# Attention and FFN on one core: one round of sums for block 3, merged score bursts in blocks 0 to 2, and a new load order for batch 3

## The chip, the cores and the metric

The kernel runs on one core of a Trainium2 chip. The metric is device time in microseconds (us), the median of several executions. Before the change it is 512.24 us (three runs, 511.84 to 512.57). The state of a run of one core is told by its time against the fastest of the same kernel.

## The reference

Two stages, cut to what matters. Shapes: q, k, v are 8 batches x 8 heads x 1024 tokens x 64; E and F are 64 x 1024; the FFN is 512 to 2048 to 512.

```python
k_proj = einsum('ks,bhsd->bhkd', E, k)       # project 1024 keys to 64
v_proj = einsum('ks,bhsd->bhkd', F, v)
scores = q @ k_proj.T / sqrt(64)             # softmax over the 64
attn   = softmax(scores) @ v_proj
x      = attn.transpose(0, 2, 1, 3).reshape(8192, 512)
h      = x @ w_in                            # ... the FFN
out    = (h * sigmoid(1.702 * h)) @ w_out
```

## The kernel before

The 8192 tokens are 16 blocks of 512, two blocks a batch. TensorE runs the FFN of block j without a break; the attention of later blocks is put into gaps of that stream: "slot n" is the gap after FFN1 group n (of 16), "O+n" the gap after FFN2 half group n (of 8). Both write to accumulation buffers: f_ps and x_ps are two sets of four. The small matmuls of the attention use the array as eight tiles of 64 rows by 32 columns:

```python
def eight(outs, lhsTs, rhss):                # 8 small matmuls, one array full
    for i, ro in ((0, (LO, HI)), (1, (HI, LO))):
        for c in range(0, KP, 32):
            for ri, r in zip((LO, HI), ro):
                nc.tensor.matmul(outs[i][r.start + c:r.start + c + 32], ...)
```

Blocks 0 to 2 are normalised token by token (`tok`). Block 3 is normalised with sums spread over the partitions by matmuls (`norm`: two sets of eight and two reciprocals for each half). Later blocks make the sums of all heads in one set (`sums`), and a trip through DRAM spreads the reciprocals (`spread`), after which `values` multiplies:

```python
def spread(h):
    def go():
        rdr = dram.tile([HP, 2, TB], F32, name="rdr")
        nc.sync.dma_start(out=rdr, in_=rdens.pop(h)[0:P:32])
        rbc[h] = att.tile([P, HP, TB], F32, name="rbc")
        for e, r in enumerate((LO, HI)):     # 2 x 512 KB
            nc.sync.dma_start(out=rbc[h][r], in_=rdr[None, :, e, :].to_broadcast([D, HP, TB]))
```

There are two streams of transfers. GpSimd issues the bulk loads, batch by batch, in the order k, q, v (1 MB each as they land; batch 1: k, v, q), each as soon as its buffer is free; k of the next batch has to wait until this batch's projection (`proj`) has read its own. SyncE issues the DMA transposes of q (`q_dma`, 1 MB) and of the projected k (in `kv_out`), the trips and the stores of the output, in program order in one queue.

The softmax here doesn't subtract the row's maximum and nothing guards it: scores larger than these inputs give would overflow.

## Time and profile before

| reading | value |
|---|---|
| time, median | 512.24 us |
| span of the profiled run | 510.4 us |
| TensorE busy | 99%, granted clock 1.000 |
| chain that ended last | TensorE 94%, DMA 4% (the start) |
| DMA engines | mean busy share 9 tenths or more in each of the first 13 slices of 12.8 us |

The page and the chain are shown in the prediction. This is the timeline of SyncE in the kernel before; the columns are start, us, engine, line, operation. For a DMA the time is how long the issue holds the queue, not how long the data moves.

```profile
111.39 6.72 SPq L252 DMA_TRANSPOSE qT<-q_sb  x1
121.81 1.17 SPq L221 DMA_TRANSPOSE kt<-k_b  x1
```

The transpose of q of batch 3 goes out at 111.39 us and holds the queue for 6.72 us; the transpose of its projected k follows at 121.81, as soon as VectorE has written it. Their reader, the scores of block 6, comes at 138.96 us.

### The profile page before, as it was taken

Reading aid. Unit: us, or ns where it says so; the run is one execution under the profiler, and the core shown is the slowest. Engines: PE = TensorE matmul, PEld = TensorE weight load, DVE = VectorE, ACT = ScalarE, POOL = GpSimd, SP = SyncE. Lnnn points to the kernel's source line nnn. Section 1 sums busy time; section 2 is a strip of 40 time slices with the busy share of each in tenths; the row PEclk is TensorE's granted clock in tenths of the full one; section 3 lists DMA queues with packets and bytes.
Section 4 is the critical chain, followed back from the end, with each engine's and each line's share of the span. In section 5 each row is a group of like instructions: output and inputs, shape, how many; then the busy total and the mean of one; then the engine's idle time right before and its main releaser. Section 6 shows DMA issues by size and latency. Waiting matters only on the chain.

```text
span 510.4 us, 7234 instructions
## 1 busy us (share of the span) xinstructions
PE 504.4 (99%) x3090; PEld 232.0 (45%) x3090; DVE 165.6 (32%) x221; ACT 264.3 (52%) x443; POOL 78.1 (15%) x97
## 2 busy tenths in 40 slices
PE   8999999999999999999999999999999999999997
PEld 4684444444444444444444444444444444444444
DVE  5513114765161623216161341616214161611000
ACT  2675564555637456471746637374563737244351
POOL 7442051514200051000510033000000000000000
PEclk9999999999999999999999999999999999999999
DMA  9999999999999099651998249990603205050202
GB/s 172 197 203 207 212 140 165 225 177 138 166 239 211 1 209 187 144 129 39 213 167 202 49 99 212 116 241 1 171 1 74 93 9 157 1 166 1 82 1 82
DMA packets 124752, 67.64 MB, mean 133 GB/s; under 512 B 92288, under 2 KB 116096, under 8 KB 122800
## 3 DMA queue, kind: packets, MB, share of 16 engines
q0 software_dynamic: 84400, 29.37, 51.4%
q1 hardware_dynamic: 40240, 37.56, 29.3%
q8 instruction: 24, 0.39, 0.3%
q10 hardware_dynamic: 80, 0.26, 0.2%
q14 instruction: 8, 0.07, 0.0%
HBM read 71.83 MB, written 16.97 MB: 174 GB/s over the span
## 4 chain that ended last, share of the span: by engine, by line
PE 94%; DMA 4%; POOL 1%; issue 0%; DVE 0%; ACT 0%; POOLq 0%
PE f_ps L405 43%; PE f_ps L373 43%; PE f_ps L165 3%; DMA w_in_sb<-in_moe_w_in_dram 2%; PE f_ps L262 2%; DMA v_sb<-in_v_dram 2%; PE x_ps L262 1%; PE x_ps L297 1%; POOL k_sb L57 0%; PE x_ps L359 0%; PE x_ps L344 0%; PE f_ps L397 0%; PE f_ps L244 0%; POOL q_sb L57 0%; POOL v_sb L57 0%
## 5 line engine op out<-in xcount | busy, mean ns | idle before, releaser
L405 PE MATMUL f_ps<-w_out_sb,gT 128*128 128x512 bf16 x1008 | 227.2, 379 | 0.0
L373 PE MATMUL f_ps<-xT,w_in_sb 128*128 128x512 bf16 (+1 forms) x1088 | 226.4, 367 | 0.3 <-DMA w_in_sb<-in_moe_w_in_dram 0.2
L376 ACT ACTIVATE gT<-f_ps 128x512 bf16<-128x512 f32 (+1 forms) x270 | 151.8, 574 | 61.4 <-PE f_ps L373 60.2
L373 PEld LDWEIGHTS <-w_in_sb 128*128 128x128 bf16 x1088 | 105.3, 98 | 116.2 <-issue 1.7
L405 PEld LDWEIGHTS <-gT 128*128 128x128 bf16 x1008 | 95.6, 98 | 120.5 <-issue 11.3
L408 ACT COPY o_sb<-f_ps 128x512 f32<-128x512 f32 x63 | 37.0, 587 | 126.8 <-PE f_ps L405 117.0
L332 DVE TENSOR_TENSOR xT<-x_ps,rbc 128x512 bf16<-128x512 f32 x48 | 30.9, 686 | 201.3 <-PE x_ps L262 124.9
L300 DVE RECIPROCAL rden<-x_ps 128x512 f32<-128x512 f32 x24 | 78.7, 3322 | 10.3 <-PE x_ps L297 10.3
L63 POOL DMA_DIRECT2D q_sb<-in_q_dram x56 | 49.1, 901 | 52.0 <-DMA k_sb<-in_k_dram 39.2
L278 ACT ACTIVATE expT<-f_ps 128x512 bf16<-128x512 f32 (+1 forms) x68 | 35.1, 571 | 32.7 <-PE f_ps L262 32.6
L57 POOL DMA_DIRECT2D k_sb<-in_k_dram x10 | 8.4, 846 | 175.5 <-PE f_ps L165 159.1
L219 DVE CAST k_b<-f_ps 64x512 bf16<-64x512 f32 x7 | 4.8, 683 | 46.8 <-PE f_ps L165 46.8
L278 ACT ACT_TABLE_LOAD x13 | 16.7, 1283 | 4.7 <-PE f_ps L262 4.5
L282 ACT ACT_TABLE_LOAD x14 | 18.0, 1283 | 0.2
L322 DVE RECIPROCAL rdn<-x_ps 128x512 f32<-128x512 f32 x4 | 13.4, 3353 | 0.8 <-PE x_ps L262 0.8
L165 PE MATMUL f_ps<-k_sb,eft 128*64 128x512 bf16 x56 | 13.4, 382 | 0.0
L165 PE MATMUL f_ps<-v_sb,eft 128*64 128x512 bf16 x56 | 13.4, 381 | 0.0
L399 DVE COPY o_sb<-f_ps 128x256 f32<-128x256 f32 x1 | 0.4, 424 | 38.6 <-issue 38.6
L135 PE MATMUL x_ps<-zeros 128*128 128x512 bf16 x34 | 11.2, 450 | 1.2 <-DVE zeros L106 1.2
L262 PE MATMUL f_ps<-qT,kt 64*32 64x512 bf16 x240 | 12.3, 386 | 0.0
L262 PE MATMUL x_ps<-expT,vq 64*32 64x512 bf16 x208 | 10.2, 377 | 0.0
L262 PEld LDWEIGHTS <-kt 64*32 64x32 bf16 x272 | 3.9, 88 | 13.7 <-issue 13.5
(71 smaller groups left out, 128.4 us busy)
## 6 DMA issues: line engine op xcount, KB each, us to landing
out_dram<-o_sb SPq DMA_DIRECT2D x15, 1024.0 KB
rbc<-rdr SPq DMA_DIRECT2D x24, 512.0 KB
k_sb<-in_k_dram POOLq DMA_DIRECT2D x7, 1024.0 KB, 13.3
v_sb<-in_v_dram POOLq DMA_DIRECT2D x7, 1024.0 KB, 10.6
q_sb<-in_q_dram POOLq DMA_DIRECT2D x56, 128.0 KB, 12.0
w_in_sb<-in_moe_w_in_dram POOLq DMA_DIRECT2D x8, 256.0 KB, 12.2
w_out_sb<-in_moe_w_out_dram POOLq DMA_DIRECT2D x4, 512.0 KB, 14.7
out_dram<-o_sb SPq DMA_DIRECT2D x3, 256.0 KB
```

Source lines behind the costliest of these rows:

```text
L63: nc.gpsimd.dma_start(out=qt[b][:, j], in_=qv[:, j])
L165: nc.tensor.matmul(kvps[b][r], eft(j, slice(e * KP, (e + 1) * KP)), (kt, vt)[e][b][:, :, j, :], start=(j == 0), stop=(j == J - 1))
L262: nc.tensor.matmul(outs[i][r.start + c:r.start + c + 32], lhsTs[i][ri, c:c + 32], rhss[i][ri], start=True, stop=True)
L278: nc.scalar.activation(expT[h][:, 2 * u + i, ts], s_ps[i], AF.Exp, scale=scale)
L282: nc.scalar.preload_act_table(AF.Gelu_apprx_sigmoid)
L300: nc.vector.reciprocal(rden[:, e, :], d_ps[e])
L322: nc.vector.reciprocal(rd, d_ps[i])
L332: nc.vector.tensor_tensor(x_of(h)[:, 2 * u + i, :], n_ps[i], rbc[h][:, 2 * u + i, :], op=ALU.mult)
L373: nc.tensor.matmul(h_ps, w_in_sb[:, kc, fc * P:(fc + 1) * P], xT[j][:, kc, ts], start=(kc == 0), stop=(kc == KC - 1))
L376: nc.scalar.activation(gts[j][:, fc, ts], h_ps, AF.Gelu_apprx_sigmoid)
L405: nc.tensor.matmul(o_ps[n], gts[j][:, fc, n * P:(n + 1) * P], w_out_sb[:, fc, :], start=(fc == 0), stop=(fc == FC - 1))
L408: nc.scalar.copy(osb[j][:, n, :], o_ps.pop(n))
```

## The change

Its intent: fewer small matmuls (one round of sums for block 3 in place of two), fewer changes between the big and the small tiling of the array (both halves of a block's scores in one burst, the second half into x_ps so that the FFN keeps its f_ps buffers), and, because block 3's reciprocals now take a trip through DRAM in the middle of the loads of batch 3, v of batch 3 ahead of its q, with a second buffer for q.

```diff
+    def q_buf(order):
+        return ldpool.tile([P, J * H * D], BF16, name="q_sb", bufs=2).rearrange(...)
     def load(b):
         load_kv(k, kt, b, "k_sb")
-        if b == 1:
+        if b in (1, 3):
             load_kv(v, vt, b, "v_sb")
         load_q(b)
-        if b > 1:
+        if b not in (1, 3):
             load_kv(v, vt, b, "v_sb")
 ...
-    def scores(h, u, half=None):
+    def scores(h, u, half=None, x=False):
 ...
-            s_ps = [f_tile([P, n * P]) for _ in range(2)]
+            s_ps = [(x_tile() if x else f_tile([P, TB]))[:, :n * P] for _ in range(2)]
 ...
-        at(0, Q + u, scores(1, u))
+        at(0, Q, scores(1, u, None, u > 0))
 ...
-        at(1, O + u, scores(2, u))
-        at(1, O + 3 + u, scores(3, u))
-        at(2, O + 2 * u, scores(4, u))
+        at(1, O, scores(2, u, None, u > 0))
+        at(2, O, scores(4, u, None, u > 0))
+        at(2, O + 3 * u, values(3, u))
 ...
+    for u in range(2):
+        at(1, O + 6, scores(3, u, None, u > 0))
 ...
-    at(2, 0, proj(2), kv_out(2))
-    at(2, 1, norm(3, 0))
-    at(2, 11, norm(3, 1))
+    at(2, 1, proj(2), kv_out(2), sums(3), spread(3))
     at(2, O, q_dma(3))
-    at(2, O + 4, scores(5, 0))
+    at(2, O + 3, scores(5, 0))
```

More of the change, by code (lines that the diff above doesn't have):

```diff
@@ L57, in load_kv @@
             nc.gpsimd.dma_start(out=dst[b][:, h:h + n, js:js + jn], in_=sv[:, h:h + n, js:js + jn])
+    def q_buf(order):
+        return ldpool.tile([P, J * H * D], BF16, name="q_sb", bufs=2).rearrange(
+            f"p ({order} d) -> p {order} d", d=D, h=H)
     def load_q(b):
-        qt[b] = ldpool.tile([P, J, H, D], BF16, name="q_sb")
+        qt[b] = q_buf("j h")
         qv = q[b].rearrange("h (p j) d -> p j h d", p=P)
@@ L85 @@
     make_identity(nc, ident)
-    load_kv(q, qt, 0, "q0_sb", H, 0, 2)
+    qt[0] = q_buf("h j")
+    load_kv(q, qt, 0, "", H, 0, 2)
     load_kv(v, vt, 0, "v_sb", ((0, 4), (4, 2), (6, 2)))
-    load_kv(q, qt, 0, "q0_sb", H, 2, 2)
+    load_kv(q, qt, 0, "", H, 2, 2)
     for i in range(6):
         load_w_in(i)
-    load_kv(q, qt, 0, "q0_sb", H, JB, JB)
+    load_kv(q, qt, 0, "", H, JB, JB)
     for i in range(6, 8):
@@ L263, in eight, with x_tile @@
                                      start=True, stop=True)
-    def scores(h, u, half=None):
+    def x_tile():
+        return ps_x.tile([P, TB], F32, name="x_ps")
+    def scores(h, u, half=None, x=False):
         b, c = divmod(h, NB2)
@@ L448 @@
     order = [(half, fc) for fcs in (range(12), range(12, FC)) for half in range(2) for fc in fcs]
-    at(0, 0, scores(0, 0, 1))
-    at(0, 1, scores(0, 1, 1), gelu_table)
+    at(0, 1, scores(0, 0, 1), scores(0, 1, 1, True), gelu_table)
     for p in range(HP):
@@ L472 @@
         at(1, O + 3 + p, x_tr(2, p, 0), x_tr(2, p, 1))
-    at(1, O + 5, gelu_table)
+    for u in range(2):
+        at(1, O + 6, scores(3, u, None, u > 0))
+    at(1, O + 6, gelu_table)
     at(1, O + 4, q_dma(2))
-    at(2, 0, proj(2), kv_out(2))
-    at(2, 1, norm(3, 0))
-    at(2, 11, norm(3, 1))
+    at(2, 1, proj(2), kv_out(2), sums(3), spread(3))
     at(2, O, q_dma(3))
-    at(2, O + 4, scores(5, 0))
+    at(2, O + 3, scores(5, 0))
     at(2, O + 6, proj(3), kv_out(3), scores(5, 1), sums(4), spread(4))
```

## The prediction

> **What bounds the kernel now.** I read the page first, then the chain of work that ended last in order of time, then the timelines of TensorE, VectorE and the DMA queue of SyncE around blocks 0 to 3 (a block is 512 tokens: 16 groups of FFN1 at L373, then 8 half groups of FFN2 at L405; "O+n" is the gap after FFN2 half group n, "slot n" the gap after FFN1 group n).
>
> ```profile
> span 510.4 us, 7234 instructions
> ...
> PE 504.4 (99%) x3090; PEld 232.0 (45%) x3090; DVE 165.6 (32%) x221; ACT 264.3 (52%) x443; POOL 78.1 (15%) x97
> ...
> DMA  9999999999999099651998249990603205050202
> ...
> PE 94%; DMA 4%; POOL 1%; issue 0%; DVE 0%; ACT 0%; POOLq 0%
> ```
>
> TensorE has work 99% of the span at full clock, and the chain is 94% TensorE; the 4% DMA is the start. So a microsecond counts only if TensorE spends it in its own stream, or waits. The DMA row has a second thing to watch: it is at 9 up to 166 us (13 slices of 12.8 us), so any transfer added before that is added to a full system.
>
> ```profile
> 40.36 0.34 PE f_ps L262 x8
> 40.70 1.83 PE f_ps L405 x8
> 42.53 0.34 PE f_ps L262 x8
> ...
> 92.35 0.56 PE x_ps L262 x16
> 92.90 8.74 PE f_ps L373 x40
> ...
> 105.75 1.73 PE f_ps L405 x8
> 107.48 0.34 PE f_ps L262 x8
> 107.82 3.56 PE f_ps L405 x16
> ...
> 121.03 0.34 PE f_ps L262 x8
> 121.37 0.22 PE x_ps L297 x8
> 121.58 1.83 PE f_ps L405 x8
> ```
>
> These rows of the chain (start, us, what) give the prices. Eight FFN matmuls take 1.73 us when they follow their own kind. Eight small matmuls (64 rows by 32 columns of the array, L262 scores and values, L297 sums) take 0.22 us when they follow other small ones, which is one pass of 512 columns for all eight. After FFN matmuls they take 0.34, and the FFN row after them takes 1.83. So **one visit to the small tiling costs 0.12 us going in and 0.10 coming back, 0.22 in all**, as much as the eight matmuls themselves. The last three rows show that what shares a visit pays once.
>
> **What the Trainium skill says.** "TensorEngine Tiling (Array Packing)", section Key Properties: "Changing tiling mode (not just tile) drains the TensorE". The trace agrees: the 0.12 and 0.10 above appear only at changes. "DMA: Bandwidth & Descriptors", section Queues, rings and completion order: each DMA engine alternates between the queues that have work for it, a packet at a time. That bears on what a small hardware-queue transfer suffers beside bulk loads; the trace shows it as the 18.4 against 9.4 us below. "Perfetto Trace Analysis", section Identifying the Most-Contended Engine, warns that TensorE's busy share does not say how near the limit it is; here I use it only for gaps, and take savings from durations in the chain.
>
> **The change, part by part.**
>
> Fewer matmuls. Block 3's normalisation (norm, two halves) is 4 sets of eight small matmuls: sums for each half, values for each half. It becomes one set for the sums (sums) and two for the values (values). The built program's order confirms 16 TensorE rows fewer (8 weight loads, 8 matmuls): one pass, 0.22 us. VectorE also loses two 128x512 reciprocals at 3.35 us, but it is busy 32% and not on the chain: worth nothing directly.
>
> Fewer visits to the small tiling, counted in blocks 0 to 2:
> - Block 0, FFN1 part: the second half of block 0's scores, two visits to one.
> - Block 0, FFN2 part: scores of block 1, two to one: saves 0.22.
> - Block 1: scores of blocks 2 and 3 were four visits (O, O+1, O+3, O+4), now two (O, O+6): saves 0.44.
> - Block 2, before: norm at slots 1 and 11, each 0.56+0.10, sum 1.32; scores at O, O+2, O+4, each 0.34+0.10, sum 1.32. After: the sums sit behind the projection of batch 2, which already has a change of tiling going back; from the projection's tiling into the small one costs 0.34 (the row at 121.03 follows a projection). Then O holds 24 matmuls (0.34+0.22+0.22+0.10 = 0.88), O+3 holds 16 (0.66). 2.64 becomes 1.88: saves 0.76, with the 0.22 of the lost pass inside it.
>
> The first item I count as **nothing**. TensorE arrives early at 27.5 us and waits for the sixth piece of w_in, the only FFN1 wait shown there:
>
> ```profile
> 27.51 4.98 PE L373 MATMUL f_ps<-xT,w_in_sb 128*128 128x256 bf16 x44 [0.20 <-DMA w_in_sb<-in_moe_w_in_dram]
> ```
>
> The loads of the start are not reordered, so that landing stays, and 0.22 us saved before it only lengthens the wait. The exps of block 0 come some 0.4 us later than now, which the same wait takes up.
>
> Sum: 0.22 + 0.44 + 0.76 = 1.42 us. 512.24 - 1.42 = 510.8. Everything after block 2 has the same instructions as now, moved earlier by 1.4 us.
>
> Moves that cost nothing, if on time. ScalarE now does four exps in a row (4 x 0.545) and a table load (1.28) at the end of block 1, 3.9 us after the burst begins; FFN1 of block 2 has the 1.9 us projection among its first three groups, so the four f_ps buffers suffice by my count. The second pair of scores goes to x_ps, so FFN2 keeps its f_ps.
>
> **The rivals.**
>
> 1. The new wait: block 3's reciprocals now go through DRAM (rdr, then rbc, 1 MB) as those of later blocks do, in the middle of the load of batch 3. What that takes in the kernel before:
>
> ```profile
> 129.31 0.62 SPq L307 DMA_DIRECT2D rdr<-rden  x1
> 134.75 1.35 SPq L310 DMA_DIRECT2D rbc<-rdr  x2
> ...
> 147.70 1.29 DVE L332 TENSOR_TENSOR xT<-x_ps,rbc 128x512 bf16<-128x512 f32 x2 [1.55 <-DMA rbc<-rdr]
> ...
> 207.74 0.55 SPq L307 DMA_DIRECT2D rdr<-rden  x1
> ...
> 217.09 1.29 DVE L332 TENSOR_TENSOR xT<-x_ps,rbc 128x512 bf16<-128x512 f32 x2 [9.38 <-DMA rbc<-rdr]
> ```
>
> It is 18.4 us beside a batch load, 9.4 later. The projection of batch 2 ends at 91.5 in the new kernel, kv_out takes VectorE 1.6, two reciprocals 6.6, so rdr goes out at 99.7 and rbc lands between 109 and 118. Who needs it: the built program's waits say that values of the second half (O+3) take x_ps buffers freed by ScalarE, not by VectorE, so TensorE does not wait there. It waits at O+6, where the sums of block 4 take the buffers of the first half's values (121.37 - 1.4 = 120.0), and at FFN1 of block 3 (about 121.8), which needs all four multiplies. 118.1 + 1.3 = 119.4 and 120.7: even the slow precedent just fits, with about 0.6 us to spare. Should it take 3 us longer, TensorE loses 2 to 3 and the time is 511.8 to 514.
>
> 2. The loads of batch 3. Now k, q, v; v lands at 116.6 (issued at 105.97, 10.6 us to landing) and its projection starts at 119.1. rbc would eat that slack of 2.5 us, and moving v ahead of q repairs it: v then lands around 113 to 116 against a projection at 117.7. But q lands last, near 118 to 121, and its transpose stands in SyncE's queue before the transpose of k and block 4's rdr. It holds the queue some 6.7 us (the one issued at 111.39 did). If q lands at 118, rdr of block 4 leaves on time at 127.5; if at 121 or later, 2 us late, and the x_ps buffers at O+6 of block 3, which now have 1.5 us to spare (multiply done at 149.0, TensorE there at 150.5), make TensorE wait 0.5 to 2 us: 511.3 to 513. I give 1 in 5 to a wait over 0.5 us from rivals 1 and 2 together.
>
> 3. The visits cost less than they seem (ends of matmuls are modelled in the profile), and only the pass of eight is saved: 512.0. Against it: the same 0.12 and 0.10 appear at every change in the chain, and the starts of the rows are recorded. 1 in 10.
>
> 4. The start: if TensorE were late at 27.5 because of the later exps, up to 0.4 us is lost; if the w_in landing is earlier by chance, as much is won. Both are within the spread of the three runs (0.7 us).
>
> **Range and chances.** Point 510.9: the 510.8 of the sum plus a little for rivals 1 and 2. The low end, 510.2, is the sum plus the first block's 0.22 and half of the runs' spread; the high end, 512.7, is the sum plus 2 us of waiting. Two per cent is 10.2 us. To gain that the kernel would have to lose seven times the waste that I found; to lose it a wait of 11 us would have to appear where the slow precedent gives none. Faster 0.01, within 0.98, slower 0.01.
>
> **What would show it.** Right: 3082 matmuls on TensorE; in the chain, rows of 24 small matmuls near 105.8 at about 0.78 us and of 16 near 112 at 0.56; FFN1 of block 3 starting near 122.0 instead of 123.42, and the whole lead of 1.4 us kept to the end. The wait for w_in at 27.5 longer, not gone. Wrong: TensorE idle with rbc, a VectorE multiply or v as its releaser between 110 and 155; FFN rows after visits shorter than 1.83 everywhere or the merged rows longer than their parts; block 4's multiply later than 149.

## The result, and the profile after

The changed kernel takes 517.98 us (median of four runs, 516.68 to 519.78) against 512.4 us for the kernel before (four runs). The ratio is 1.0109, with a 95% interval from 1.0072 to 1.0146. Ratios here and below are the mean time of one kernel's fast runs over that of the other's fast runs of the same rounds, so not quite the ratio of the medians. It is slower by 1.1%, outside the predicted range of 510.2 to 512.7.

The page of the changed kernel, its general lines:

```profile
span 514.9 us, 7152 instructions
...
PE 498.7 (97%) x3031; PEld 232.1 (45%) x3082; DVE 158.4 (31%) x219; ACT 264.0 (51%) x443; POOL 78.0 (15%) x97
...
PEclk9999999999989999999999999999999999999999
...
PE 91%; DMA 6%; issue 1%; POOL 1%; SPq 0%; DVE 0%; ACT 0%; POOLq 0%
```

TensorE fell from 99% to 97% busy and the DMA part of the chain rose from 4% to 6%. One slice has a lower clock, which no slice of the kernel before has. (3082 weight loads are the 8 fewer that the change removes; some matmul records are missing, so 3031 is no count.)

The chain of the changed kernel from block 3 on, in order of time (start, us, what). FFN1 is now L381, FFN2 L413:

```profile
122.09 9.93 PE f_ps L381 x46
...
133.33 0.67 SPq L257
...
134.06 7.16 DMA kt<-k_b
...
141.26 0.63 PE f_ps L267 x8
...
143.07 11.12 PE f_ps L413 x47
154.20 0.34 PE f_ps L267 x8
```

The same stretch of the chain before:

```profile
138.96 0.34 PE f_ps L262 x8
...
139.73 10.47 PE f_ps L405 x48
150.19 0.34 PE f_ps L262 x8
```

FFN1 of block 3 starts at 122.09 us instead of 123.42: **the lead of 1.33 us is there**. Then the chain leaves TensorE, for SyncE (L257, the transpose of q) and for the DMA that transposes k, and comes back at 141.26. From the start of FFN1 to the scores of block 6 it took 15.54 us before and takes 19.17 now: 3.63 us lost. From there to the scores at O+6 it took 11.23 and takes 12.94: 1.71 more, although nothing waits there. Up to FFN1 of block 4 another 0.18 goes (2.79 against 2.61). -1.33 + 3.63 + 1.71 + 0.18 = 4.19 us. FFN1 of block 4 starts at 156.99 instead of 152.80, and the last instruction at 511.44 instead of 507.25: 4.19 us both times. **All that was lost was lost between 122 and 157 us.** (The profiled run is the fastest of the four.)

The wait itself, in the list of who waited for whom (line, releaser: total, times, longest):

```profile
PE f_ps L267 <- DMA kt<-k_b: 3.6, 1, 3.6
```

SyncE's and GpSimd's timelines of the changed kernel say why that transpose was late:

```profile
104.60 1.32 SPq L318 DMA_DIRECT2D rbc<-rdr  x2
120.79 13.21 SPq L257 DMA_TRANSPOSE qT<-q_sb  x1
134.06 1.29 SPq L226 DMA_TRANSPOSE kt<-k_b  x1
```

```profile
110.94 0.88 POOL L67 DMA_DIRECT2D q_sb<-in_q_dram  x1 [5.33 <-DMA v_sb<-in_v_dram]
120.29 0.87 POOL L57 DMA_DIRECT2D k_sb<-in_k_dram  x1 [8.47 <-PE x_ps L305]
```

The last piece of q of batch 3 is issued at 110.94 (104.76 before) and lands 9.7 us later, at 120.6. Its transpose starts at 120.79 instead of 111.39. In that moment, at 120.29, GpSimd starts the loads of batch 4, and the transpose holds SyncE's queue for 13.21 us instead of 6.72. The transpose of k, whose input VectorE has written by 120.45, goes out at 134.06, lands at 141.2, and TensorE, which wanted it at 137.6, sits idle.

The 1.71 us is the clock. These rows of the table by stretch (stretch, us, busy time of TensorE, weight loads, VectorE, ScalarE and GpSimd, granted clock, DMA share, GB/s) are of the kernel before and of the changed one:

```profile
141.20:145.00 3.80, 3.80 (x19) 1.75 (x18) 3.80 (x2) 1.04 (x3) 0.00 (x0) 1.00 1.15 268
```

```profile
141.20:145.00 3.80, 3.41 (x30) 1.20 (x32) 2.62 (x1) 2.37 (x3) 0.00 (x0) 0.55 1.72 186
```

The clock averages 0.55 in the 3.8 us after the gap, a loss of 3.8 x 0.45 = 1.71 us. The Trainium skill, "TensorE: Matmul & The Clock Gate", section What's actually happening, has the array's clock drop to half after an idle window of about 3.4 us. The trace agrees in kind: 3.6 us of idling cost 1.7 us more.

### The profile page after: what moved, and what is told of

Its sections match the earlier page's. It is cut to its first block, busy times and chain, and to the rows that moved or that the text cites. A ratio compares the mean times of both kernels' runs of the same rounds, so it can differ in the third digit from the quotient of the medians.

```text
span 514.9 us, 7152 instructions
## 1 busy us (share of the span) xinstructions
PE 498.7 (97%) x3031; PEld 232.1 (45%) x3082; DVE 158.4 (31%) x219; ACT 264.0 (51%) x443; POOL 78.0 (15%) x97
## 4 chain that ended last, share of the span: by engine, by line
PE 91%; DMA 6%; issue 1%; POOL 1%; SPq 0%; DVE 0%; ACT 0%; POOLq 0%
PE f_ps L413 42%; PE f_ps L381 42%; PE f_ps L170 3%; DMA w_in_sb<-in_moe_w_in_dram 2%; DMA v_sb<-in_v_dram 2%; PE f_ps L267 2%; PE x_ps L267 1%; DMA kt<-k_b 1%; PE x_ps L305 1%; POOL k_sb L57 0%; PE x_ps L352 0%; PE x_ps L367 0%; PE f_ps L405 0%; PE f_ps L249 0%; POOL q_sb L57 0%
## 5 line engine op out<-in xcount | busy, mean ns | idle before, releaser
L381 PE MATMUL f_ps<-xT,w_in_sb 128*128 128x512 bf16 (+1 forms) x1072 | 225.0, 366 | 1.5 <-ACT gT L384 0.3
L413 PE MATMUL f_ps<-w_out_sb,gT 128*128 128x512 bf16 x975 | 221.6, 380 | 4.2 <-issue 3.7
L381 PEld LDWEIGHTS <-w_in_sb 128*128 128x128 bf16 x1088 | 105.4, 98 | 116.1 <-issue 0.9
L413 PEld LDWEIGHTS <-gT 128*128 128x128 bf16 x1008 | 96.2, 98 | 122.5 <-issue 13.4
L416 ACT COPY o_sb<-f_ps 128x512 f32<-128x512 f32 x63 | 37.0, 587 | 132.2 <-PE f_ps L413 121.1
L340 DVE TENSOR_TENSOR xT<-x_ps,rbc 128x512 bf16<-128x512 f32 x52 | 33.4, 686 | 219.0 <-PE x_ps L267 120.9
L308 DVE RECIPROCAL rden<-x_ps 128x512 f32<-128x512 f32 x26 | 85.3, 3323 | 14.5 <-PE x_ps L305 14.4
L286 ACT ACTIVATE expT<-f_ps 128x512 bf16<-128x512 f32 (+1 forms) x58 | 30.1, 573 | 29.9 <-PE f_ps L267 29.8
L267 PE MATMUL f_ps<-qT,kt 64*32 64x512 bf16 x208 | 10.9, 394 | 3.6 <-DMA kt<-k_b 3.6
L359 DVE TENSOR_TENSOR x_sb<-x_ps,rd 128x256 bf16<-128x256 f32 x22 | 9.3, 425 | 0.8
```

Of the source, the lines that this page charges most:

```text
L267: nc.tensor.matmul(outs[i][r.start + c:r.start + c + 32], lhsTs[i][ri, c:c + 32], rhss[i][ri], start=True, stop=True)
L286: nc.scalar.activation(expT[h][:, 2 * u + i, ts], s_ps[i], AF.Exp, scale=scale)
L308: nc.vector.reciprocal(rden[:, e, :], d_ps[e])
L340: nc.vector.tensor_tensor(x_of(h)[:, 2 * u + i, :], n_ps[i], rbc[h][:, 2 * u + i, :], op=ALU.mult)
L381: nc.tensor.matmul(h_ps, w_in_sb[:, kc, fc * P:(fc + 1) * P], xT[j][:, kc, ts], start=(kc == 0), stop=(kc == KC - 1))
L413: nc.tensor.matmul(o_ps[n], gts[j][:, fc, n * P:(n + 1) * P], w_out_sb[:, fc, :], start=(fc == 0), stop=(fc == FC - 1))
```

## The experiments

The first theory (A) was that v ahead of q is what makes q late. Its rival (B) was that the trip does the harm, whatever the order. After the first four runs theory C replaced both. In all runs the outputs were correct.

### Batch 3 loaded in the order k, q, v again

```diff
-        if b in (1, 3):
+        if b == 1:
             load_kv(v, vt, b, "v_sb")
         load_q(b)
-        if b not in (1, 3):
+        if b > 1:
```

> The changed kernel with the loads of batch 3 back in the order k, q, v (q keeps its own buffer). Theory A (v ahead of q makes q land late, so its transpose holds SyncE's queue until 134 us and the transpose of k and TensorE wait behind it): q of batch 3 lands near 113 us, its transpose is out of SyncE's queue by about 121, the k transpose follows at about 121, and the 3.6 us wait of TensorE at 137.6 us is gone; in its place v lands near 119 to 120 against a projection that wants it at 117.8, a wait of 1 to 2 us. Time 511 to 513 us. Theory B (the extra DRAM trip of block 3's reciprocals, not the order of the loads, delays the transposes): the wait for the k transpose stays, time 515 to 518.

Measured: 518.97 us, ratio 1.0128 (1.0104 to 1.0152). The wait for k's transpose is gone, as A said, but another is as long, 4.2 us instead of the expected 1 to 2:

```profile
PE f_ps L170 <- DMA v_sb<-in_v_dram: 4.2, 1, 4.2
```

The order of the loads only chooses which transfer is the late one. This run also prices the trip. In the kernel before, the landing of k lets the last piece of q go at 104.76 us, and that lands at 111.3, 6.5 us later. Here it goes at 106.08 and lands at 118.3, 12.2 us later. In between runs the trip, issued from 106.54 on and multiplied from 118.22. 1 MB of it took about 11.7 us and delayed the bulk loads by 5.7, about half of that. This agrees with the sharing by turns that the prediction cites from the skill; no run here tells it from another way of sharing.

### Only the merged bursts

The kernel before with the new `scores` and its places, without the sums, the loads and the later projection.

> The kernel before with only the scores of blocks 0 to 2 put into one burst each (no change of block 3's sums, none of the loads). If one visit to the small tiling costs 0.22 us, three visits fewer on TensorE's path (block 1's, 2's, 3's and 4's scores: one in block 0, two in block 1, one in block 2, so four; the one before 27.5 us is hidden) save 0.88 us: 511.4 to 511.7, no wait of TensorE between 40 and 160 us. If the visits are an artefact of the modelled ends of matmuls: 512.2 to 512.6.

Measured: 512.07 us, ratio 0.9995 (0.9981 to 1.001). The bursts are shorter as expected (block 2 starts at 87.67 us instead of 88.47; starts of a timeline lie up to 0.2 us before those of the chain), but the lead stops at the next load, v of batch 2:

```profile
PE f_ps L165 <- DMA v_sb<-in_v_dram: 0.7, 1, 0.7
```

FFN1 of block 3 starts at 123.24 us, against 123.25 in the timeline of the kernel before. So a TensorE that arrives earlier wins nothing where a load lands just in time. The whole change puts this projection one slot later, and there, as in the held versions below, no such wait is seen.

### Only the loads of batch 3

The kernel before with q's second buffer and v ahead of q.

> The kernel before with only q's second buffer and v of batch 3 ahead of its q. Theory A: the order alone makes q land some 7 us later (118 instead of 111), its transpose meets the loads of batch 4 and is out of the queue at about 130, the k transpose lands at 137 to 139 just when TensorE wants it at 139: 512.5 to 515 us. Theory B: without the DRAM trip of block 3's reciprocals the transpose is on time, 512.2 to 512.6.

Measured: 512.42 us, ratio 1.0004 (0.9986 to 1.0021). Theory A fell here, and the time is that of theory B. From the timelines of SyncE and GpSimd:

```profile
118.51 4.78 SPq L257 DMA_TRANSPOSE qT<-q_sb  x1
123.39 1.19 SPq L226 DMA_TRANSPOSE kt<-k_b  x1
```

```profile
123.14 0.87 POOL L57 DMA_DIRECT2D k_sb<-in_k_dram  x1 [10.41 <-PE x_ps L302]
```

q's transpose does start some 6 us later (118.51, in a run whose block 2 already starts 1.4 us later), but it holds the queue for 4.78 us only: it is through at 123.3, when the loads of batch 4 start (123.14). No wait of TensorE was added in this stretch.

### q of batch 3 first

The changed kernel with the order q, k, v, which the second buffer makes possible.

> The changed kernel with batch 3's loads in the order q, k, v: q's own buffer is free long before k's, so q can be issued right behind v of batch 2. Theory A: q lands near 100 us, its transpose goes out right behind the DRAM trip of block 3's reciprocals at about 106 and is done before batch 4's loads start; no wait for the k transpose; v lands near 116 to 119, a wait of at most 1 us at the projection. 510.7 to 512 us, faster than the kernel before. Theory B: still a wait of some 3 us, 514 to 518.

Measured: 517.60 us, ratio 1.0100 (1.0083 to 1.0118), a miss for A. The time is that of theory B, but the wait is for v, not for k's transpose. q's transpose went out early, at 107.79 us, but held the queue for 14.97 us beside the loads of k and v, and v came late:

```profile
PE f_ps L173 <- DMA v_sb<-in_v_dram: 3.5, 1, 3.5
```

Three orders of the same transfers, three waits of 3.5 to 4.2 us. That gave **theory C**: with the trip, the transfers up to about 126 us no longer fit; something is late in any order, and a DMA transpose is slow beside bulk loads. The engines are not full without a break: in the changed kernel the DMA share is 0.04 from 120 to 122 us, around the landing of q. What meets there is q's transpose and the loads of batch 4, issued within 0.5 us of each other.

### The loads of batch 4 held back

```diff
+    hold = consts.tile([P, 1], BF16, name="hold")
+    at(3, 14, lambda: nc.gpsimd.tensor_copy(hold, gts[3][:, 13, :1]))
```

GpSimd cannot go on to the loads of batch 4 before it has copied one element of a GELU result of block 3. Nothing else differs from the changed kernel.

> The changed kernel with the loads of batch 4 held back on GpSimd until GELU 13 of block 3 (about 134 us; they are wanted at 179). Theory C (the DMA engines are full: the transpose of batch 3's q is slow, 13.2 us instead of 6.7, because batch 4's loads start in the same moment): the transpose takes 5 to 7 us, the k transpose is out by 128 and lands by 130, no wait at 137.6 us; 510.7 to 511.7 us, a little faster than the kernel before. Theory D (the transpose is slow whatever runs beside it, for instance because of where q's second buffer lies): 13 us again, 516 to 519.

Measured: 511.10 us (511.02 to 511.20), ratio 0.9961 (0.994 to 0.9983). SyncE's queue:

```profile
121.31 4.96 SPq L257 DMA_TRANSPOSE qT<-q_sb  x1
126.32 1.24 SPq L226 DMA_TRANSPOSE kt<-k_b  x1
```

q lands as late as in the changed kernel, but with the engines free its transpose takes 4.96 us instead of 13.21. TensorE has no wait in this stretch, the clock is 1.000, and the time is that of the prediction's sum. Theory C holds, and D falls.

### Block 3's normalisation as before, all else changed

> The changed kernel with block 3's normalisation as before (norm at slots 1 and 11, no trip through DRAM), all other parts kept: bursts, q's buffer, v ahead of q, batch 2's projection one slot later. Theory C (the 1 MB trip is what overfills the DMA engines): no wait of TensorE between 85 and 160 us, and the visits saved show: 511.1 to 511.6 us. If the trip is not the cause: 515 to 518.

Measured: 512.06 us, ratio 0.998 (0.9958 to 1.0001). Without the trip there is no long wait, as C says. The gain is smaller than expected, and its interval touches 1: of a lead of 0.85 us at the start of block 2 (87.62 against 88.47) 0.41 is left at the sums behind the projection (91.87 against 92.28), which waits for v of batch 2 (0.2 us in the list of waits), and a set of values in the second half of `norm` takes 0.86 us instead of 0.40, which uses up the rest. The chain of this run shows what the second waited for: the last of these matmuls start at 101.86, right behind VectorE's multiply of the first half, which ends at 101.82. In the kernel before it ends at 101.24, before these matmuls start (101.80). VectorE is later here because the projection, one slot later and held up by v, ends at 91.96 instead of 91.38.

### The trip alone, added to the kernel before

```diff
+    def trip(h, parts):
+        def go():
+            t = att.tile([P, HP, TB], F32, name="rbc")
+            for r in (LO, HI)[:parts]:
+                nc.sync.dma_start(out=t[r], in_=E[None, :HP, :TB].to_broadcast([D, HP, TB]))
+        return go
-    at(2, 1, norm(3, 0))
+    at(2, 1, norm(3, 0), trip(3, 2))
```

> The kernel before with nothing changed but two more DMA copies on SyncE at slot 1 of block 2, of the size and shape of one reciprocals' trip (2 x 512 KB broadcast into an rbc tile that nobody reads). Theory C: they take half of the engines' turns for some 12 us, v of batch 3 lands 4 to 6 us later than 116.6 and the projection at 119.1 waits 2 to 4 us; 514.5 to 517. If the trip hurts only through its own wait chain and not by its bytes: 512.2 to 512.7.

Measured: 514.43 us (514.37 to 514.56) against a median of 512.63; ratio 1.0026 (1.0 to 1.0051), where the kernel before had one run at 514.81 that pulls its mean up. v of batch 3 landed at 121.1 us instead of 116.6, 4.5 later:

```profile
PE f_ps L165 <- DMA v_sb<-in_v_dram: 1.3, 1, 1.3
```

So bytes that nobody reads are enough to make TensorE wait. Time and wait are a little under what was expected. The clock did not drop after a gap of 1.3 us.

### The trip in bf16

> The changed kernel with reciprocals in bf16 on their whole way (rden, rdr, rbc), which halves the bytes of every trip. Theory C: q of batch 3 lands some 3 us earlier, at 117 to 118, its transpose is well under way when batch 4's loads start, and the wait for the k transpose shrinks from 3.6 to between 0 and 1.5 us: 511 to 514. Were bytes not the matter: 516 to 519.

Measured: 516.00 us, ratio 1.0059 (1.0022 to 1.0095), a miss, and not a clean test. The wait for k's transpose is gone, but the tile pool gave the second half of `values` other buffers, those of its first half, so that TensorE waits for the multiply, which waits for the trip:

```profile
114.72 0.40 PE L267 MATMUL x_ps<-expT,vq 64*32 64x512 bf16 x4 [3.08 <-DVE xT L341]
```

After these 3.1 us the clock is 0.68 in the next 3.3 us and 0.84 in the 4.0 after them. The delay also moved the loads of batch 4 to 125.3 us, so q's transpose (4.96 us) had the engines to itself for that reason as well. What half the bytes would bring stays open.

### k's transpose ahead of q's in SyncE's queue

```diff
-    at(2, O, q_dma(3))
-    at(2, O + 6, proj(3), kv_out(3), scores(5, 1), sums(4), spread(4))
+    at(2, O + 6, proj(3), kv_out(3), q_dma(3), scores(5, 1), sums(4), spread(4))
```

> The changed kernel with the transpose of batch 3's q put behind that of its k in SyncE's queue (it was ahead of it). If only the order in SyncE's queue does the harm: the k transpose goes out at 121 us, the q transpose is out by 134 and its data is in before 137.6, no wait, 511 to 512. Theory C (the transposes crawl beside batch 4's loads): the q transpose, issued at about 122 to 135, lands at 139 to 141 and TensorE waits 2 to 4 us for it in place of k's; 515 to 518.

Measured: 517.25 us, ratio 1.0109 (1.0062 to 1.0156). k's transpose went out at 120.40. q's held the queue for 12.81 us, and TensorE waited for that one instead:

```profile
PE f_ps L267 <- DMA qT<-q_sb: 3.5, 1, 3.5
```

This is what theory C expected; the order in SyncE's queue is not the cause either.

### A shorter hold

As the held version, with the copy at slot 6, from GELU 5.

> The held version with the loads of batch 4 freed earlier, after GELU 5 of block 3 (about 127.5 us) instead of GELU 13 (134.9). Theory C says that what matters is to keep them off the engines until the two transposes are out of the queue at 126 to 127.5: no wait of TensorE, 511.0 to 511.3, like the longer hold. If the hold helps by giving the trip of block 4's reciprocals (from 128 us) free engines: that trip is slow again, TensorE waits at O+6 of block 3, 512 to 515.

Measured: 510.89 us (510.56 to 511.80), ratio 0.997 (0.9952 to 0.9989). GpSimd starts the loads at 128.74, just behind the two transposes (4.93 us from 120.53; k's at 125.51), and nothing waits. The long and the short hold are equal within their spread. Both beat both kernels: by 1.5 us the kernel before, by some 7 us the changed one.

## Why the prediction was wrong

**Right: the sum.** The visits saved and the pass saved were worth 1.33 us at the start of block 3's FFN1 (1.42 predicted); with the disturbance removed, the kernel came out at 511.10 and 510.89 us, against 510.8 of the sum: 1.5 and 1.6 us under the kernel before in the same rounds, where 1.42 was predicted. The merged bursts took 0.77 us (24 small matmuls at 105.96, 0.78 predicted) and 0.56 us (16 at 112.02, as predicted). The doubt of rival 3, that the visits are an artefact of the profile, is answered by these times. That the first burst before 27.5 us brings nothing was not tested apart; in the chains FFN1 goes on behind the landing of w_in at 27.69 us, against 27.51 before.

**Right: rival 1.** rdr went out at 99.98 us and the multiplies started at 116.26, 16.3 us later, between the two precedents. TensorE waited for none of it, as the built program's waits said.

**Wrong: the step of rival 2.** The prediction had the mechanism by name (q lands last, its transpose holds SyncE's queue) and even q's landing (118 to 121; it was 120.6). The step that failed is "It holds the queue some 6.7 us (the one issued at 111.39 did)". It held it for 13.21 us. The precedent had been taken while one bulk load was in flight; 9.4 us later the same instruction stood beside the start of batch 4's loads. The transpose of 1 MB took 4.8 to 5.0 us in five runs where the engines were free or nearly so, and 6.2 to 15.0 beside bulk loads; what decides between 6.2 and 15.0 was not tested. From this followed a second miss: I checked block 4's reciprocals as the victim, and the first one was the transpose of k, for the scores of block 6, 20 us after the late landing.

**Missing: two terms.** The price of the trip to others (5.7 us of the bulk loads' time, where the prediction had only set it against v's slack of 2.5 us) and the clock after a gap (1.71 us). With a wait of 3.6 us they turn a gain of 1.4 into a loss of 4.2 in the profiled run. The chance of 1 in 5 for a wait over 0.5 us, and the top of the range at 2 us of waiting, were too mild for a change that adds a transfer to engines at 9 tenths.

**Half right: the order of the loads.** "Moving v ahead of q repairs it" is true of v (no wait at the projection). It does not lower the total, and the debt fell on q. The load order alone, without the trip, was harmless.

## What to carry to other kernels

When the DMA engines are full over a stretch, count what a new transfer takes from the others there, not only when it lands itself: reordering moves the wait from one tensor to the next, and only taking bytes out or moving a load into a stretch with room ends it. Here one tiny instruction that holds the next batch's loads back for 8 us turned a loss of 1.1% into a gain of 0.3%. A duration taken from the trace holds for the neighbours it was measured with: before moving an instruction by 10 us, look at what starts there, and follow its delay to every reader.

## What the Trainium skill lacked or had wrong

- "TensorEngine Tiling (Array Packing)", Key Properties, says that a change of tiling drains TensorE but gives no price. Here a visit to the 64x32 tiling cost 0.12 us going in and 0.10 coming back, as much as the 0.22 us of the eight matmuls themselves.
- "Perfetto Trace Analysis", section DMA Instruction — HWDGE, has the profiled window of such a DMA end when its descriptors are generated, and data movement outside it. It does not say that the window grows when the engines are busy: the same 1 MB transpose held SyncE's queue for 4.93 us with free engines and for 13.21 us beside bulk loads.
- "TensorE: Matmul & The Clock Gate", section What's actually happening, puts the drop of the clock at an idle window of about 3.4 us; the table in its section Why this matters for your kernels warns of gaps over about 3 us, which fits better here. A gap of 3.1 us was followed by a clock of 0.68 in the next 3.3 us and one of 3.6 us by 0.55 in the next 3.8, while one of 1.3 us had no effect. The loss (length of a stretch times what its clock lacks to 1) adds up to some 1.7 us after the gaps of 3.1, 3.6 and 4.2 us and after that of 3.5 us for q's transpose, but to 3.3 us after the one of 3.5 us in the run with q first.
